# Attention and a gated FFN on one core: a planned order made anew, and queries loaded without their zeros

## Chip, cores and metric

The kernel runs on one core of a Trainium2 chip. The metric is the device time of one execution in microseconds. A core has five engines that run their own instruction streams and meet at semaphores: TensorE (PE in the profile, with its weight loads as PEld), VectorE (DVE), ScalarE (ACT), GpSimd (POOL) and SyncE (SP), which here only issues DMAs.

## What is computed

Two stages, all in float32. First a chunked attention over 4 batches, 8 heads, 768 positions and head size 64. Each chunk of 32 queries sees 16 positions to its left, its own 32, 8 to its right, and 8 memory keys shared by the head, so 64 keys. Then a feed-forward stage (FFN) with a gate: 512 to 1024 columns, ReLU, a convolution over three neighbouring positions, a sigmoid of it as the gate, and 1024 back to 512 columns.

```python
for c in range(nc):                      # 24 chunks of 32 queries
    k_full = concat([mem_k, k_ctx]); v_full = concat([mem_v, v_ctx])
    scores = scale * q_c @ k_full.T
    scores = scores - max(scores)
    a = exp(scores); a = a / (sum(a) + 1e-09)
    out[c] = a @ v_full
...
h = maximum(x @ w_in, 0.0)
conv_out = sum(conv_w[k] * hp[:, k:k + S, :] for k in range(3))
gate = 1.0 / (1.0 + exp(-conv_out))
return (h * gate) @ w_out
```

The FFN's weights come as float64, which the kernel reads as pairs of 32-bit words.

## The kernel before, in words

**An order written by a planner.** The function `attention_then_gated_ffn` doesn't emit instructions as it goes. It hands every operation to a `Plan` (`plan.op`, line 63): the engine, an assumed cost in ns, a due time, the code that emits it, what it reads and writes, and sometimes an ACT table (`exp` or `sigmoid`) or a mode of TensorE (`tiled` for the small matmuls of the attention, `whole` for the rest). `Plan.run` (line 99) then goes through time: of all operations that could start on an engine within a nanosecond of the earliest, it takes the one with the smallest due time, with `SWITCH` added where the operation needs another table than the one loaded and `MODE` where it changes TensorE's mode (line 150). It emits them in that order, one in-order stream for each engine and one for SP's DMA queue. The due times come from the table `DUE` (line 34): a start and a step for each group of operations. Costs and due times only set the order; what makes an instruction wait on the chip are its true dependences. Tiles come from rings of a few buffers each (`tile_of`, line 232), and a tile is handed out only when the planner has seen the last use of the buffer before it.

**Attention.** There are 32 steps `n` of the function `attention` (line 346): batch, half of the positions (`hf`, 12 chunks) and pair of heads (`cc`). One step: three loads (q, k, v), then 12 score matmuls of 64 stationary columns by 64 keys, one per chunk (line 384). Each stands in the profile as two instructions, so that a step has 24. The stationary operand holds a block diagonal: rows 0 to 63 are the first head and have its 32 queries in columns 0 to 31, rows 64 to 127 are the second head with columns 32 to 63, and the rest is zero. These zeros are in the array in device memory: `q_d` is loaded as 128 rows of 12 x 64 numbers (384 KB), with the 64 columns of a chunk side by side. Two chunks run beside each other in two column halves of the array (`j`). Then softmax: maximum on VectorE (line 393), subtract on VectorE (395), exp on ACT (397), edges set to zero (401, 403), sum, 1e-9 and reciprocal on VectorE (406 to 408), and the normalising product on GpSimd (413). Three transposes on TensorE (418), two copies by ACT into the block diagonal `a_d` (429), 12 matmuls with v (437, again two instructions each), and the result is split into a high and a low part, `x_hi` by ACT (446) and `x_lo` by VectorE (449). The first four steps take their q and k tiles from the ring `h`, later ones from rings of two.

**Weights.** `from_f64` (line 255) makes a high and a low float32 part of 128 x 512 float64 numbers. It has three recipes, chosen by a letter per block in `W_IN` and `W_OUT` (line 32): M works on VectorE (7 operations) and ACT, C on VectorE (6), ACT and one product on GpSimd, R on VectorE (4), ACT and three operations on GpSimd (316, 320, 325).

**FFN.** `ffn_in` (line 472 for its matmuls) takes, for each of 8 blocks of 128 hidden columns and each half of the positions, 12 matmuls of 384 columns; ACT applies the ReLU (488). `gate` (492) works per block on 128 x 768: the first tap of the convolution on ACT (498) or VectorE (502), two more on VectorE (508), the sigmoid on ACT (512), the product with h on VectorE or GpSimd (516). `split` (522) makes a high part by ACT (526) and a low part by VectorE or GpSimd (529). `ffn_out` (547) has 24 matmuls of 512 columns for each of 6 blocks of 128 positions and each batch, then a copy by ACT (559) and the store.

**Which engine does what.** Batch 0 has its first tap on ACT, and its product and low part in turn on GpSimd and VectorE. The other batches have tap and product on VectorE and the low part on GpSimd. All attention steps subtract on VectorE and normalise on GpSimd.

Of the kernel before, what the change touches and what calls it, by code (L numbers as in the profile page):

```python
# [22 lines left out]
NH = 2  # L23
NC = 12
# [3 lines left out]
TINY = 1.75 * 2.0**-15  # L28
WC = 512


W_IN, W_OUT = "MRRRCRMM", "MMRCMRMM"

DUE = {
    "w_in": (-1.1, 2.25), "w_in_load": (-15.9, 3.07), "w_out": (90, 0.44), "w_out_load": (55.6, 5.48),
# [4 lines left out]
    "gate": (25.7, 5.17)  # L40
# [10 lines left out]
class Plan:  # L51
# [47 lines left out]
    def run(self):  # L99
# [23 lines left out]
        for _ in range(n):  # L123
# [77 lines left out]
SWITCH, MODE = 1.9, 6.7  # L201
# [3 lines left out]
def attention_then_gated_ffn(  # L205
# [41 lines left out]

    w_in_p = [const.tile([P, NFC, NCC, P], F32R, name=f"w_in_{p}") for p in ("hi", "lo")]
# [6 lines left out]
    def from_f64(src, hi, lo, key, n, kind, due, first):  # L255

        w = tile_of("w64", 4, [P, WC, 2], U32)
# [88 lines left out]
    def attention(n, due):  # L346

        b, r = divmod(n, NU)
        hf, cc = divmod(r, NCC)

        q_d, k_t = (tile_of(*(("h", NFC) if n < 4 else (x, 2)), y) for x, y in (("q_d", [P, NC, 2 * CH]), ("k_t", [P, KC])))
        v_t = tile_of("v_t", 3, [P, NG, 2, 2, D])
        s, e, top, z = bank("s", 2), tile_of("e", 3, [P, 2 * NG, KW]), *(tile_of(x, 4, [P, 2 * NG]) for x in ("top", "z"))
# [4 lines left out]
        W = 2 * NG * KW  # L358
        s_ = lambda: s.t[:, :W].rearrange("p (g k) -> p g k", k=KW)
        over = lambda y: y.t.unsqueeze(2).broadcast_to([P, 2 * NG, KW])  # L360

        def load(tile, src, ahead):
            size = 1
            for x in src.shape:
                size *= x
            def do():
                flat = tile.t
                if len(flat.shape) == 3:
                    flat = flat.rearrange("p c q -> p (c q)")
                if len(flat.shape) == 5:  # L370
                    flat = flat.rearrange("p g c h d -> p (g c h d)")
                nc.sync.dma_start(out=flat, in_=src)
            plan.op("DMA", size * 4 / 300, due - DUE["load"][0] + ahead, do, w=(tile,))

        load(q_d, q[b, hf, cc], 0)
        load(k_t, k[b, hf, cc], 0)
        load(v_t, v[b, hf, cc], 1)

        def scores():
            for g in range(NG):  # L380
                for p in range(2):
                    for j in range(2):
                        c = 4 * g + 2 * j + p
                        nc.tensor.matmul(
                            s_()[j * D : (j + 1) * D, 2 * g + p, :],
                            lhsT=q_d.t[:, c],
                            rhs=k_t.t[:, c * STEP : c * STEP + KW],
                            start=True,
                            stop=True,
                        )  # L390

        plan.op("PE", 24 * 30, due, scores, (q_d, k_t), (s,), mode="tiled", late=250)
        plan.op("V", vec(W), due, lambda: nc.vector.tensor_reduce(out=top.t, in_=s_(), axis=AX.X, op=ALU.max), (s,), (top,))  # L393
        plan.op(
            "V", vec(W), due, lambda: nc.vector.tensor_tensor(out=e.t, in0=s_(), in1=over(top), op=ALU.subtract), (s, top), (e,)  # L395
        )
        plan.op("A", act(W), due, lambda: nc.scalar.activation(e.t, e.t, AF.Exp, scale=SCALE), (e,), (e,), table="exp")  # L397


        if hf == 0:  # L400
            plan.op("V", 80, due, lambda: nc.vector.memset(e.t[:D, 0, :LEFT], 0.0), (), (e,))
        if hf == NH - 1:
            plan.op("V", 80, due, lambda: nc.vector.memset(e.t[D:, 2 * NG - 1, KW - RIGHT :], 0.0), (), (e,))

        def total():
            nc.vector.tensor_reduce(out=z.t, in_=e.t, axis=AX.X, op=ALU.add)  # L406
            nc.vector.tensor_scalar_add(out=z.t, in0=z.t, scalar1=1e-9)  # L407
            nc.vector.reciprocal(out=z.t, in_=z.t)  # L408

        plan.op("V", vec(W) + 350, due, total, (e,), (z,))  # L410
        plan.op(
            "G", 2.15 * W, due,
            lambda: nc.gpsimd.tensor_tensor(out=e.t, in0=e.t, in1=over(z), op=ALU.mult), (e, z), (e,), shared=True,  # L413
        )

        def turn():
            for g in range(NG):
                nc.tensor.transpose(  # L418
                    out=t.t[:, g * P : (g + 1) * P],
                    in_=e.t[:, 2 * g : 2 * g + 2].rearrange("p g k -> p (g k)"),  # L420
                    identity=ident,
                )

        plan.op("PE", NG * 109, due, turn, (e,), (t,), mode="whole", late=250)
        for p in range(2):
# [5 lines left out]
            plan.op("A", act(W, True), due, place, (t,), (("a_d", p),))  # L431
# [155 lines left out]
    for n in range(4):  # L587
        attention(n, T_ATT[n])
# [3 lines left out]
    for n in range(4, 8):  # L592
        attention(n, T_ATT[n])
    tokens_in(0, (1,), *DUE["in0b"])
    for n in range(8, 12):
        attention(n, T_ATT[n])
    tokens_in(1, (0,), *DUE["in1a"])
    for n in range(12, 16):
        attention(n, T_ATT[n])
# [12 lines left out]
    y = [gate(fc, hs[1, fc][0], lin("gate1", fc), "V", "V", True) for fc in range(NFC)]  # L612
    g = [split(*y[fc], lin("split1", fc), "G") for fc in range(NFC)]
    for n in range(16, 24):
        attention(n, T_ATT[n])
    t = DUE["out"][0]
    def out_rest(b, g, t, last):
        for tt in range(3):
            ffn_out(b, g, tt, [t + 2.1 * fc + 0.1 * tt for fc in range(NFC)])
        for tt in range(3, 6):  # L620
            ffn_out(b, g, tt, [t + 17 + 5.7 * (tt - 3) + 0.7 * fc for fc in range(NFC)], 2 if last and tt == 5 else 1)
    out_rest(1, g, t, False)
    t += 34 + 8
    for b in range(2, B):
        tokens_in(b, (0, 1), t, 4.2)
        g = []
        for fc in range(NFC):
            y = gate(fc, hs[b, fc][0], t + lin("gate", fc), "V", "V")
            g.append(split(*y, t + lin("gate", fc), "G"))
        if b + 1 < B:  # L630
            for n in range((b + 1) * NU, (b + 2) * NU):
                attention(n, T_ATT[n])
# [6 lines left out]
def _laid_out(q, k, v, mem_k, mem_v):  # L639
# [19 lines left out]

    qt = q.reshape(B, H // 2, 2, NH, NC, CH, D).transpose(0, 3, 1, 2, 6, 4, 5)  # L660
    ql = np.zeros((B, NH, H // 2, 2, D, NC, 2, CH), q.dtype)
    for h in range(2):
# [50 lines left out]
```

## Time and profile before

| | |
|---|---|
| median of 3 runs | 371.07 us (370.65 to 371.46) |
| the profiled execution | 370.88 us |
| span of its instructions | 369.0 us |
| mean granted clock of TensorE in it | 0.982 |
| moved by DMA | 48.62 MB |
| ACT table loads | 22 of 1.283 us each |

The span runs from the first to the last instruction on the chip; the execution's time has 1.9 us around it. In the profile, "busy" of an engine is the time in which it had at least one instruction under way. Matmuls overlap one another, and the duration of a single one contains its latency: how fast they follow is read from the distance of their starts, not from their duration. "Idle before" of a group is time in which the engine stood empty just ahead of these instructions, and the name behind it is what released it.

### The profile page before, as it was taken

Reading aid. Unit: us, or ns where it says so; the run is one execution under the profiler, and the core shown is the slowest. Engines: PE = TensorE matmul, PEld = TensorE weight load, DVE = VectorE, ACT = ScalarE, POOL = GpSimd, SP = SyncE. Lnnn points to the kernel's source line nnn. Section 1 sums busy time; section 2 is a strip of 40 time slices with the busy share of each in tenths; the row PEclk is TensorE's granted clock in tenths of the full one; section 3 lists DMA queues with packets and bytes.
Section 4 is the critical chain, followed back from the end, with each engine's and each line's share of the span. In section 5 each row is a group of like instructions: output and inputs, shape, how many; then the busy total and the mean of one; then the engine's idle time right before and its main releaser. Section 6 shows DMA issues by size and latency. Waiting matters only on the chain.

```text
span 369.0 us, 7477 instructions
## 1 busy us (share of the span) xinstructions
PE 343.3 (93%) x3000; PEld 303.3 (82%) x3000; DVE 273.5 (74%) x444; ACT 212.4 (58%) x353; POOL 122.2 (33%) x155
## 2 busy tenths in 40 slices
PE   1577999999999999969999999999999999999996
PEld 1456999899999988857767899998868799998786
DVE  4979999999999999999995016999972117888300
ACT  4465777798755643879666127577594216453311
POOL 1665521244424354333542102254333002443300
PEclk9957999999999999999999999999999999999999
DMA  8988776844664000455643500413612100000021
GB/s 295 404 295 283 250 252 233 287 121 165 215 198 159 0 0 2 158 185 172 195 147 103 197 28 2 124 63 116 224 46 90 59 28 2 0 0 2 6 108 59
DMA packets 19907, 48.62 MB, mean 132 GB/s; under 512 B 2336, under 2 KB 6688, under 8 KB 19872
## 3 DMA queue, kind: packets, MB, share of 16 engines
q1 hardware_dynamic: 19872, 48.14, 38.1%
q8 instruction: 24, 0.39, 0.4%
q14 instruction: 11, 0.09, 0.1%
HBM read 41.84 MB, written 6.29 MB: 130 GB/s over the span
## 4 chain that ended last, share of the span: by engine, by line
DVE 54%; PE 28%; issue 6%; ACT 6%; POOL 3%; DMA 1%; POOLq 1%; DVEq 0%; ACTq 0%
PE f L547 16%; DVE c L508 14%; PE f L472 8%; DVE c L516 4%; DVE c L502 4%; DVE z L406 3%; DVE e L395 3%; DVE w_top L288 3%; DVE z L407 3%; DVE top L393 3%; PE a L437 3%; DVE x_lo L449 2%; DVE w L302 2%; DVE w_top L281 2%; DVE w L309 2%
## 5 line engine op out<-in xcount | busy, mean ns | idle before, releaser
L547 PE MATMUL f<-w_out_hi,g 128*128 128x512 f32 (+1 forms) x400 | 127.7, 392 | 0.3 <-POOL g L529 0.2
L472 PE MATMUL f<-x_hi,w_in_hi 128*128 128x384 f32 x256 | 89.1, 348 | 0.0
L547 PEld LDWEIGHTS f<-w_out_hi,g 128*128 128x128 f32 x400 | 74.0, 188 | 17.4 <-POOL g L529 1.6
L472 PE MATMUL f<-x_lo,w_in_hi 128*128 128x384 f32 x256 | 86.5, 338 | 0.0
L472 PE MATMUL f<-x_hi,w_in_lo 128*128 128x384 f32 x256 | 86.4, 338 | 0.0
L547 PE MATMUL f<-w_out_lo,g 128*128 128x512 f32 (+1 forms) x200 | 77.0, 385 | 0.0
L529 POOL TENSOR_TENSOR g<-c,g 128x768 fp32r<-128x768 f32 x20 | 40.4, 2018 | 96.1 <-ACT g L526 92.3
L508 DVE SCALAR_TENSOR_TENSOR c<-h,cw,c 128x768 f32<-128x768 f32 x48 | 62.2, 1296 | 1.6
L413 POOL TENSOR_TENSOR e<-e,z 128x384 f32<-128x384 f32 x32 | 30.0, 940 | 71.1 <-DVE z L408 26.3
L472 PEld LDWEIGHTS f<-x_hi,w_in_hi 128*128 128x128 f32 x256 | 48.6, 190 | 1.0
L472 PEld LDWEIGHTS f<-x_hi,w_in_lo 128*128 128x128 f32 x256 | 48.6, 190 | 0.1
L472 PEld LDWEIGHTS f<-x_lo,w_in_hi 128*128 128x128 f32 x256 | 48.4, 189 | 0.0
L547 PEld LDWEIGHTS f<-w_out_lo,g 128*128 128x128 f32 x200 | 37.6, 188 | 7.1
L502 DVE TENSOR_SCALAR c<-h,cw 128x768 f32<-128x768 f32 x24 | 21.7, 905 | 25.3 <-ACT h L488 25.3
L488 ACT ACTIVATE h<-f 128x384 f32<-128x384 f32 x48 | 23.5, 490 | 26.1 <-PE f L472 25.8
L437 PEld LDWEIGHTS a<-a_d,v_t 128*64 128x64 f32 x768 | 26.6, 144 | 12.9 <-issue 6.4
L512 ACT ACTIVATE c<-c 128x768 f32<-128x768 f32 x32 | 27.1, 846 | 17.0 <-DVE c L508 16.8
L559 ACT COPY o_sb<-f 128x512 f32<-128x512 f32 (+1 forms) x25 | 14.0, 569 | 38.0 <-PE f L547 26.6
L437 PE MATMUL a<-a_d,v_t 128*64 128x64 f32 x768 | 30.9, 233 | 4.5 <-ACT a_d L429 2.6
L429 ACT COPY a_d<-t 64x384 f32<-64x384 f32 x64 | 30.2, 472 | 5.8 <-PE t L418 5.1
L449 DVE TENSOR_TENSOR x_lo<-a,x_hi 128x384 fp32r<-128x384 f32 x32 | 17.3, 542 | 16.3 <-ACT x_hi L446 16.1
L397 ACT ACTIVATE e<-e 128x384 f32<-128x384 f32 x32 | 16.8, 524 | 20.7 <-DVE e L395 19.8
(63 smaller groups left out, 439.9 us busy)
## 6 DMA issues: line engine op xcount, KB each, us to landing
v_t<-in_v_dram SPq DMA_DIRECT2D x32, 384.0 KB, 3.7
q_d<-in_q_dram SPq DMA_DIRECT2D x28, 384.0 KB, 5.2
k_t<-in_k_dram SPq DMA_DIRECT2D x28, 252.0 KB, 5.3
out_dram<-o_sb SPq DMA_DIRECT2D x23, 256.0 KB, 2.0
w<-in_w_in_dram SPq DMA_DIRECT2D x8, 512.0 KB, 5.1
w<-in_w_out_dram SPq DMA_DIRECT2D x8, 512.0 KB, 4.0
h<-in_q_dram SPq DMA_DIRECT2D x4, 384.0 KB, 6.4
h<-in_k_dram SPq DMA_DIRECT2D x4, 252.0 KB, 6.4
```

The costliest lines, as they stand in the source:

```text
L397: plan.op("A", act(W), due, lambda: nc.scalar.activation(e.t, e.t, AF.Exp, scale=SCALE), (e,), (e,), table="exp")
L413: lambda: nc.gpsimd.tensor_tensor(out=e.t, in0=e.t, in1=over(z), op=ALU.mult), (e, z), (e,), shared=True,
L429: nc.scalar.copy(out=a_d[r, :, p, :], in_=t.t[r, : NG * P].rearrange("p (g q) -> p g q", q=CH))
L437: nc.tensor.matmul(a.t[h * D : (h + 1) * D, g * P + j * D : g * P + (j + 1) * D], lhsT=v_t.t[:, g, j, h], rhs=a_d[:, 4 * g + 2 * j + h].re ...
L449: lambda: nc.vector.tensor_tensor(out=x_lo.t[:, cc], in0=a.t[:, :TW], in1=x_hi.t[:, cc].bitcast(F32), op=ALU.subtract),
L472: nc.tensor.matmul(f.t[:, :TW], lhsT=w_in_p[c][:, fc, cc], rhs=x_p[a].t[:, cc], start=(m == 0), stop=(m == 3 * NCC - 1),)
L488: nc.scalar.activation(h.t[:, 1 + o : 1 + o + TW], f.t[:, :TW], AF.Relu)
L502: lambda: nc.vector.tensor_scalar(out=c.t, in0=h.t[:, 0:S], scalar1=w[0], scalar2=None, op0=ALU.mult),
L508: lambda i=i: nc.vector.scalar_tensor_tensor(out=c.t, in0=h.t[:, i : i + S], scalar=w[i], in1=c.t, op0=ALU.mult, op1=ALU.add), (*H, c), (c ...
L512: plan.op("A", act(S), due, lambda: nc.scalar.activation(c.t, c.t, AF.Sigmoid), (c,), (c,), table="sigmoid")
L529: lambda: (nc.vector if lo == "V" else nc.gpsimd).tensor_tensor(out=g_lo(), in0=x(), in1=g_hi().bitcast(F32), op=ALU.subtract), (h, p[0]), ...
L547: nc.tensor.matmul(ps.t[:, :n], lhsT=g[fc][a].t[:, tt * P : (tt + 1) * P], rhs=w_out_p[c][:, fc, o : o + n], start=(fc == 0 and i == 0), s ...
```

## The change

*Queries.* The zeros are no longer in device memory. `queries` loads each step's two heads as two DMAs of 64 rows, 96 KB each, into the two blocks of a tile `[P, 2, CH, NC]` whose other blocks are set to zero by GpSimd. From the fifth step on there are two such tiles, zeroed once and used in turn; the first four steps take tiles of the ring `h`, each zeroed by itself. The chunk is now the innermost index, so that the 64 stationary columns of a chunk, `q_t()[:, :, :, c]`, stand 12 numbers (48 bytes) apart.

*Softmax.* By the letters of `SOFT`, 13 of 32 steps no longer subtract on VectorE: VectorE multiplies the six maxima by -scale, and ACT does six exps of 64 columns straight from the scores' bank, with the maximum as bias. By `NORM`, 17 of 32 steps normalise on VectorE, the other 15 on GpSimd.

*Gate.* The letters of `TAP`, `MULT` and `LO` choose the engine of the first tap (24 ACT, 8 VectorE; before 8 and 24), of the product (19 GpSimd, 13 VectorE; before 4 and 28) and of the low part (12 GpSimd, 20 VectorE; before 28 and 4) for each block of each batch.

*Weights.* `W_IN` and `W_OUT` have other letters.

*Order.* All due times are new. `SWITCH` goes from 1.9 to 64.1 and `MODE` from 6.7 to 32.4, and the planner's cost for a change back to whole matmuls from 250 to 120 ns. The three operations between sum and reciprocal are separate entries now. The change also allows steps to be worked in pairs (`PAIRS`, `GROUP`), but every group has one step.

```diff
-W_IN, W_OUT = "MRRRCRMM", "MMRCMRMM"
+W_IN, W_OUT = "MRCCCCMM", "RRRRMMCC"
+TAP = "AVVAAAAVAAAAAAVAAVAVVVAAAAAAAAAA"
+MULT = "GVVVVGGVGGGGGVVVVGGVVGGGVGGGVGGG"
+LO = "GGVGVVGVVVVGGGVVVVVVVGGVVGGVVVGV"
+SOFT = "VAVVVAAAAAAAVVVAVVVVVAVVVVVAAVVA"
+NORM = "VGGGGGGGGGGVGGGGVVVVVVVVVVVVVVGV"
+GROUP = "11111111"
 DUE = {
-    "w_in": (-1.1, 2.25), "w_in_load": (-15.9, 3.07), "w_out": (90, 0.44), "w_out_load": (55.6, 5.48),
-    "load": (11.3, 6.35), "att0": (1.5, 0), "att1": (13.3, 3.09), "att2": (23.5, 4.11), "att3": (68.2, 4.75),
-    "att4": (134.9, 6.29), "att6": (222.1, 6.59), "in0a": (16.2, 1.93), "in0b": (48.4, 3.05),
-    "in1a": (66.7, 2.68), "in1b": (88.8, 1.97), "gate0": (73.5, 8.41), "out0": (103.6, 0.84),
-    "out0b": (136.8, 2.94), "gate1": (167.1, 0), "split1": (148.2, 7), "out": (169.8, 0.83),
-    "gate": (25.7, 5.17)
+    "w_in": (-0.3, 2.09), "w_in_load": (-19.8, 9.87), "w_out": (51.2, 2.77), "w_out_load": (51.2, 19.2),
+    "load": (4.9, 2.04), "att0": (-2.8, 0), "att1": (-2.5, 5.14), "att2": (27.1, 4.41), "att3": (49.2, 4.44),
+    "att4": (142.6, 7.91), "att6": (217.8, 5.47), "in0a": (22.9, 0.55), "in0b": (74.4, 0.42),
+    "in1a": (114.4, 1.22), "in1b": (120.2, 1.59), "gate0": (71.8, 6.93), "out0": (151.7, 0.66),
+    "out0b": (138.3, 0), "gate1": (133.1, 5.76), "split1": (124.6, 12.08), "out": (192.1, 2.65),
+    "gate": (68.9, 9.63)
 }
...
-                cost += 95 if md == "tiled" else 250
+                cost += 95 if md == "tiled" else 120
...
-SWITCH, MODE = 1.9, 6.7
+PAIRS = False
+SWITCH, MODE = 64.1, 32.4
...
+    q_d = [const.tile([P, 2, CH, NC], F32, name=f"q_d{i}") for i in range(2)]
+    for x in q_d:
+        nc.gpsimd.memset(x[:D, 1], 0.0)
+        nc.gpsimd.memset(x[D:, 0], 0.0)
...
+                def less(i=i, s_=s_):
+                    for g in range(2 * NG):
+                        nc.scalar.activation(
+                            part(e, i)[:, g], s_()[:, g], AF.Exp, bias=part(top, i)[:, g : g + 1], scale=SCALE
+                        )
...
+            plan.op(
+                norm, vec(W) if norm == "V" else 2.2 * W, due,
+                lambda i=i: (nc.vector if norm == "V" else nc.gpsimd).tensor_tensor(
+                    out=part(e, i), in0=part(e, i), in1=part(z, i).unsqueeze(2).broadcast_to([P, 2 * NG, KW]), op=ALU.mult
+                ), ((e, i), z), ((e, i),), shared=True,
+            )
...
+    def queries(n, b, hf, cc, due):
+        if n < 4:
+            tile = tile_of("h", NFC, [P, 2, CH, NC])
+            get, key = (lambda: tile.t), tile
+            def zeros():
+                nc.gpsimd.memset(tile.t[:D, 1], 0.0)
+                nc.gpsimd.memset(tile.t[D:, 0], 0.0)
+            plan.op("G", 840, due, zeros, w=((tile, 2),))
+        else:
+            get, key = (lambda: q_d[n % 2]), ("q_d", n % 2)
+        for h in range(2):
+            r = slice(h * D, (h + 1) * D)
+            plan.op(
+                "DMA", D * TW * 4 / 300, due,
+                lambda r=r, h=h: nc.sync.dma_start(out=get()[r, h].rearrange("p q c -> p (q c)"), in_=q[b, hf, cc, r]),
+                w=((tile, h),) if n < 4 else (("q_d", n % 2, h),),
+            )
...
-                            s_()[j * D : (j + 1) * D, 2 * g + p, :],
-                            lhsT=q_d.t[:, c],
+                            s.t[j * D : (j + 1) * D, o : o + KW],
+                            lhsT=q_t()[:, :, :, c].rearrange("p h q -> p (h q)"),
                             rhs=k_t.t[:, c * STEP : c * STEP + KW],
...
-        y = gate(fc, hs[0, fc][0], due, "A", "GV"[fc % 2])
-        g.append(split(*y, due, "VG"[fc % 2]))
+        g.append(split(*through_gate(0, fc, due), due, LO[fc]))
...
-    ql = np.zeros((B, NH, H // 2, 2, D, NC, 2, CH), q.dtype)
-    for h in range(2):
-        ql[:, :, :, h, :, :, h] = qt[:, :, :, h]
+    ql = q.reshape(B, H // 2, 2, NH, NC, CH, D).transpose(0, 3, 1, 2, 6, 5, 4).reshape(B, NH, H // 2, 2 * D, CH * NC)
```

More of the change, by code (lines that the diff above doesn't have):

```diff
@@ new lines, in scores, with mm @@
+    def scores(s, q_t, q_k, k_t, due):
+        def mm():
+            for g in range(NG):
+                for p in range(2):
+                    for j in range(2):
+                        c = 4 * g + 2 * j + p
+                        o = (2 * g + p) * KW
+                        nc.tensor.matmul(
+                            s.t[j * D : (j + 1) * D, o : o + KW],
+                            lhsT=q_t()[:, :, :, c].rearrange("p h q -> p (h q)"),
+                            rhs=k_t.t[:, c * STEP : c * STEP + KW],
+                            start=True,
+                            stop=True,
+                        )
+        plan.op("PE", 24 * 30, due, mm, (*q_k, k_t), (s,), mode="tiled", late=250)
@@ L348, in attention, with outcome @@
+    def outcome(n, v_t, e, i, due):
         b, r = divmod(n, NU)
         hf, cc = divmod(r, NCC)
-        q_d, k_t = (tile_of(*(("h", NFC) if n < 4 else (x, 2)), y) for x, y in (("q_d", [P, NC, 2 * CH]), ("k_t", [P, KC])))
-        v_t = tile_of("v_t", 3, [P, NG, 2, 2, D])
-        s, e, top, z = bank("s", 2), tile_of("e", 3, [P, 2 * NG, KW]), *(tile_of(x, 4, [P, 2 * NG]) for x in ("top", "z"))
         t, a = bank("t", 1), bank("a", 1)
@@ L357, in attention @@
         x_hi, x_lo = x_of[b, hf]
[L358 to L373, printed above, removed]
@@ L392, in attention @@
[L392 to L401, printed above, removed]
@@ L402, in attention @@
[L402 to L414, printed above, removed]
@@ L586, in attention_then_gated_ffn, with steps, through_gate @@
     T_ATT += [lin("att3", i) for i in range(4)] + [lin("att4", i) for i in range(8)] + [lin("att6", i) for i in range(8)]
-    for n in range(4):
-        attention(n, T_ATT[n])
+    def steps(i, n):
+        while i < n:
+            size = GROUP[i // 4] == "2" and i % 2 == 0 and 2 or 1
+            attention(range(i, i + size), T_ATT[i : i + size], SOFT[i], NORM[i])
+            i += size
+    def through_gate(b, fc, due, keep=False):
+        i = b * NFC + fc
+        return gate(fc, hs[b, fc][0], due, TAP[i], MULT[i], keep)
+    steps(0, 4)
     for fc in range(NFC):
@@ L611, in attention_then_gated_ffn @@
         ffn_out(0, g, tt, [lin("out0b", fc) + 0.1 * tt for fc in range(NFC)])
[L612 to L615, printed above, removed]
+    y = [through_gate(1, fc, lin("gate1", fc), True) for fc in range(NFC)]
+    g = [split(*y[fc], lin("split1", fc), LO[NFC + fc]) for fc in range(NFC)]
+    steps(16, 24)
     t = DUE["out"][0]
@@ L627, in attention_then_gated_ffn @@
         for fc in range(NFC):
-            y = gate(fc, hs[b, fc][0], t + lin("gate", fc), "V", "V")
-            g.append(split(*y, t + lin("gate", fc), "G"))
+            due = t + lin("gate", fc)
+            g.append(split(*through_gate(b, fc, due), due, LO[b * NFC + fc]))
         if b + 1 < B:
-            for n in range((b + 1) * NU, (b + 2) * NU):
-                attention(n, T_ATT[n])
+            steps((b + 1) * NU, (b + 2) * NU)
         out_rest(b, g, t + 34, b + 1 == B)
```

100 lines of the change are left out of this document (74 added, 26 removed).

## The prediction, made before the changed kernel was run

> **What bounds the kernel now.** I read the page first: the engines' totals and the span in forty slices.
>
> ```profile
> span 369.0 us, 7477 instructions
> PE 343.3 (93%) x3000; PEld 303.3 (82%) x3000; DVE 273.5 (74%) x444; ACT 212.4 (58%) x353; POOL 122.2 (33%) x155
> ...
> PE   1577999999999999969999999999999999999996
> ...
> DVE  4979999999999999999995016999972117888300
> ```
>
> TensorE (PE) is the engine that matters: from the fifth slice on it is nearly always busy, while VectorE (DVE) is full from the fourth to the twenty-second slice and has room after that. All work of TensorE is needed, so time can come only from its empty places, from its changes between kinds of work, or from what one piece of its work costs. To place the empty time I cut the span at the points where the kind of work changes (columns: stretch, its length, busy time of PE, PEld, DVE, ACT and POOL, then the granted clock, the DMA share and GB/s).
>
> ```profile
> 0.00:7.80 7.80, 0.00 (x0) 0.00 (x0) 3.23 (x7) 3.81 (x5) 1.38 (x7) 1.00 0.78 275
> 7.80:32.80 25.00, 15.64 (x255) 13.44 (x256) 21.14 (x55) 12.79 (x27) 14.43 (x14) 0.77 0.92 333
> 32.80:41.00 8.20, 8.19 (x101) 7.63 (x99) 7.89 (x18) 6.37 (x13) 2.71 (x7) 0.86 0.72 222
> 41.00:150.00 109.00, 108.15 (x1000) 99.65 (x997) 104.54 (x179) 72.67 (x128) 40.42 (x58) 1.00 0.46 157
> 150.00:206.00 56.00, 52.17 (x535) 40.96 (x534) 47.23 (x76) 41.12 (x61) 22.52 (x21) 1.00 0.51 172
> 206.00:346.00 140.00, 139.58 (x1012) 125.13 (x1011) 89.45 (x114) 71.60 (x114) 38.85 (x48) 1.00 0.17 57
> 346.00:369.00 23.00, 19.59 (x107) 16.46 (x105) 0.00 (x0) 4.05 (x8) 1.84 (x1) 1.00 0.19 69
> ```
>
> [...] **The start (17 us) and 150 to 206 (4 us) are all there is to win by order.** What is waited for there, by the waits view, first of 7.8 to 41 us, then of 150 to 206 us:
>
> ```profile
> PEld t L418 <- POOL e L413: 6.3, 3, 2.9
> ```
> ```profile
> PEld t L418 <- POOL e L413: 4.3, 5, 1.7
> ```
>
> In both stretches PE's largest wait (the first leaves out the first loads) is the transpose of the attention weights, waiting for the normalisation that GpSimd (POOL) does. The end of the start, from the timeline, shows an in-order queue as well:
>
> ```profile
> 31.40 0.83 POOL L413 TENSOR_TENSOR e<-e,z 128x384 f32<-128x384 f32 x1 [1.81 <-DVE w_top L281]
> 31.77 0.52 ACT L397 ACTIVATE e<-e 128x384 f32<-128x384 f32 x1 [1.53 <-DVE e L395]
> 32.28 0.90 PE L418 MATMUL t<-ident,e 128*128 128x128 f32 x3 [2.73 <-POOL e L413]
> 32.32 0.48 ACT L446 CAST x_hi<-a 128x384 fp32r<-128x384 f32 x1
> ```
>
> The last x_hi that the first FFN matmul needs comes from ACT at 32.32, behind an exp (31.77) that stood 1.53 us waiting for VectorE; PE stood 2.73 us.
>
> **The change, part by part.** The groups of instructions give the prices (columns: line, engine, operation, tiles, count | busy us, mean ns | idle before):
>
> ```profile
> L498 ACT ACTIVATE c<-g,cw 128x768 f32<-128x768 f32 x8 | 7.4, 935 | 0.1
> L502 DVE TENSOR_SCALAR c<-h,cw 128x768 f32<-128x768 f32 x24 | 21.7, 905 | 25.3 <-ACT h L488 25.3
> L395 DVE TENSOR_TENSOR e<-s,top 128x384 f32<-128x384 f32 x32 | 17.8, 555 | 1.8 <-PE t L418 0.3
> L397 ACT ACTIVATE e<-e 128x384 f32<-128x384 f32 x32 | 16.8, 524 | 20.7 <-DVE e L395 19.8 <-DVE e L401 0.6
> L488 ACT ACTIVATE h<-f 128x384 f32<-128x384 f32 x48 | 23.5, 490 | 26.1 <-PE f L472 25.8
> L294 ACT CAST cw_hi<-w_top 128x24 fp32r<-128x24 f32 x1 | 0.2, 214 | 0.0
> L413 POOL TENSOR_TENSOR e<-e,z 128x384 f32<-128x384 f32 x32 | 30.0, 940 | 71.1 <-DVE z L408 26.3 <-DVE x_lo L449 9.3 <-ACT g L488 9.1
> L320 POOL TENSOR_TENSOR w_top<-w_top,w 128x512 f32<-128x512 f32 x6 | 7.9, 1319 | 0.4
> L325 POOL TENSOR_TENSOR w_in_lo<-w_top,w_in_hi 128x512 fp32r<-128x512 f32 x4 | 5.4, 1354 | 2.5 <-ACT w_in_hi L322 2.5
> ```
>
> *Engines.* By the letters, taps on VectorE fall from 24 to 8: 16 x 0.905 = 14.5 us off DVE, 16 x 0.935 = 15.0 us onto ACT. Seventeen of 32 normalisations go from POOL to DVE: 17 x 0.94 = 16.0 us off POOL, and 17 x 0.555 (the subtract of the same shape) = 9.4 us onto DVE. The two 768-wide products of the gate only change places: 32 on POOL before, 31 after. Thirteen steps take max off inside ACT's exp: 13 x 0.555 = 7.2 us off DVE, less a scaling of six columns, which I take at the 0.21 us of the smallest row here, and six activations of 64 columns in place of one of 384. Between 0.214 us (24 columns) and 0.490 us (384) a 64-column one is about 0.25 us, so 1.5 us for 0.52 us, +13 us on ACT. Together DVE loses 14.5 + 7.2 - 2.8 - 9.4 = about 10 us of 273, ACT gains some 28 of 212, and POOL loses 14 to 16 of 122. ACT at 240 is still two thirds of the span; table loads, which the new SWITCH weight puts off, I leave at no change. None of this is PE time, so by itself it is worth nothing outside the stretches with empty PE.
>
> *The start.* In the first four weight blocks the recipe M R R R becomes M R C C. An R gives POOL three products, a C only the first of them: two blocks without L320 and L325 are 2 x (1.32 + 1.35) = 5.3 us less of the 14.4 us on POOL, whose products stand in line ahead of the normalisations that the transposes wait for. The first step's normalisation goes to DVE, and the due times put the first four steps (-2.8) ahead of the first weight block (-0.3), where before two weight blocks came first. Against it: step 4 is due at -2.5, also ahead of that block, and DVE is 85% busy. The queries' half saves 192 KB ahead of the first scores, at 275 GB/s 0.7 us. Best case: all 9.4 + 0.7 = 10.1 us; worst: another wait as long as the longest here, +2.9 us. I take -4.0, a little over a third of the empty time, because half the wait view's transposes (6.3 us) should go with POOL's queue and the rest hangs on DVE, which is not relieved here.
>
> *150 to 206.* All eight steps of the third batch normalise on DVE. Their 4.3 us of PE waits end with POOL's queue; the next to be late is DVE itself, busy 47 of 56 us, since here five products leave it and five subtractions of the same shape come, so that only 7 taps less 8 normalisations relieve it (7 x 0.905 - 8 x 0.555 = 1.9 us). I take -2.0 of the 3.8 us empty; bounds -3.8 and +3.8 (as much again).
>
> *Changes of kind.* The rows of the next fence show 48 score matmuls in one block from 39.55 to the next matmul at 41.05, 1.50 us, while a block of 24 alone takes 45.41 to 46.26, 0.85 us: joining two saves 0.2 us. MODE goes from 6.7 to 32.4, so more blocks should join; if five of the 64 groups of 24 join one that they didn't before, -1.0, bounds -3 and 0.
>
> *Zeros and loads.* From the timeline, POOL's one large memset, a query load and the first v loads as SP issues them, and the first matmuls that read v:
>
> ```profile
> 1.25 0.74 POOL L246 MEMSET a_d<- 128x768 f32 x1
> ...
> 1.64 0.42 SPq L372 DMA_DIRECT2D h<-in_q_dram  x1
> ...
> 7.72 1.99 SPq L372 DMA_DIRECT2D v_t<-in_v_dram  x3
> ...
> 17.74 1.30 PE L437 MATMUL a<-a_d,v_t 128*64 128x64 f32 x24
> ```
>
> Twelve half-tile memsets on POOL, half of L246 each, are 12 x 0.37 = 4.4 us. The four for the lasting tiles and the two for step 0 end 2.2 us after L246, at 4.2, before the first scores at 7.8: hidden under the loads. Without that cover each would delay the scores by 0.37. Each step has one DMA more on SP's queue, 0.42 us to issue. Behind the four extra ones of the start stand the v loads, 1.7 us later than 7.72, and those are first read at 17.74. I take 0; bound +2.
>
> *The stationary columns.* This is the price that the trace doesn't hold: in every load of weights there the columns are adjacent. The rows: blocks at full clock, the stretch around 20.5 us with its clock of 0.50 and a block in it, load groups of 64 and 128 columns, and the only strided reads there are (ACT reading every second word, L273, beside the same width unstrided, L294).
>
> ```profile
> 39.55 1.57 PE L384 MATMUL s<-k_t,q_d 128*64 128x64 f32 x48
> ...
> 41.05 0.44 PE L472 MATMUL f<-x_hi,w_in_hi 128*128 128x384 f32 x1
> ...
> 45.41 0.92 PE L437 MATMUL a<-a_d,v_t 128*64 128x64 f32 x24
> 46.26 0.44 PE L472 MATMUL f<-x_hi,w_in_hi 128*128 128x384 f32 x1
> ```
> ```profile
> 20.40:22.00 1.60, 1.52 (x25) 1.41 (x25) 1.20 (x3) 0.03 (x1) 0.19 (x1) 0.50 1.03 376
> ...
> 20.48 1.55 PE L437 MATMUL a<-a_d,v_t 128*64 128x64 f32 x24 [1.44 <-ACT a_d L429]
> ```
> ```profile
> L472 PEld LDWEIGHTS f<-x_hi,w_in_hi 128*128 128x128 f32 x256 | 48.6, 190 | 1.0
> ...
> L384 PEld LDWEIGHTS s<-k_t,q_d 128*64 128x64 f32 x672 | 22.2, 143 | 0.7 <-issue 0.7
> ...
> L273 ACT ACTIVATE w_top<-w 128x512 f32<-128x512 f32 (+1 forms) x17 | 11.1, 650 | 4.5 <-DMA w<-in_w_in_dram 3.0 <-POOL w_out_lo L325 0.5 <-POOL w_in_lo L325 0.5
> ...
> L294 ACT CAST w_out_hi<-w_top 128x512 fp32r<-128x512 f32 x6 | 3.7, 620 | 5.3 <-DVE w_top L288 5.3
> ```
>
> 64 columns more cost a load 190 - 143 = 47 ns, and matmuls on the two column halves of the array go in pairs, 1.50 us / 24 = 62 ns each: the load fits with 15 ns to spare. From below: 0, if a strided load is as fast. From above: everything at half speed, the block at half clock, 1.55 - 0.92 = 0.63 us a step, 32 x 0.63 = 20 us. The nearest row, the same load unstrided, says 0, and the strided read on ACT costs 5%, 2 ns of 47; I take **0**, and keep +20.
>
> [...]
>
> **The sum.** -4.0 - 2.0 - 1.0 = -7.0 us. The profiled execution took 370.9 us, 1.9 outside its span; the median of the runs is 371.1, so I predict **364.0**.
>
> **Rivals.** (1) *The strided load is the bound* of the score blocks. With half the rate a load takes 94 ns, and a pair about 94 instead of 62: 32 ns x 12 pairs x 32 steps = 12 us; by the half-clock block 20. A few steps lie in the start's empty time, so +15: 379. It decides once a load takes over 62 ns, and eats the whole gain at 62 + 7.0 us / 384 = 80 ns. For it: only 15 ns of cover. Against: nothing measured. Chance 0.27. (2) *The new order makes as many waits as it removes*: DVE stays over 80% busy from 8 to 200 us, ACT's six-part exp holds a score bank 1 us longer in the start, and with x as late as before the time is 370 (368 to 373). For it: PE's waits follow whichever engine is late, and 13 us more exp stand in ACT's in-order queue, which already cost 1.5 us at 31.77. Against: POOL, the releaser of the largest waits, is the engine relieved. Chance 0.20. (3) *The start is cleared better than I take*: FFN matmuls from 26 instead of 32.8, full clock with it, 357. Chance 0.08, and 0.45 for the forecast, 360 to 368.
>
> **Chances and range.** About 0.2% is what a measurement of this kernel can tell from no change. Faster: 0.45 + 0.08 + 0.08 of rival 2 + 0.02 of rival 1 = 0.63; same 0.08; slower 0.29. The forecast's own range is 359 to 368; for 8 in 10, with rival 1 up to its lower half and a little beyond, 356 to 381.
>
> **What would show it.** First FFN matmul at 28 to 29 us instead of 32.8; a PE wait for POOL's e under 3 us in the start and under 1 after 150; PE busy in the stretches from 40 us to the end close to full; a lone score block of 24 still 0.85 us and its loads 143 ns. A block of 1.2 us or more shows rival 1, and the forecast is wrong by that. An FFN start at 32 or later, or new waits for DVE and ACT of 5 us, shows rival 2.

## The result: slower by 3.3%, and the profile after

| | before | after |
|---|---|---|
| median, same chip | 371.26 us (370.65 to 371.69, 4 runs) | 383.25 us (382.94 to 385.14, 4 runs) |
| ratio after to before | | 1.0332, 95% interval 1.0299 to 1.0364 |
| the profiled execution | 370.88 us | 385.14 us |

The forecast was 364.0 with a range of 356 to 381: wrong in sign, and outside its range by 2 us. From here on the price of a part is worked out from the difference of two ratios, each to the kernel before on the same chip, times 371.3 us; after is then +12.3 us. Times and ratios are of fast runs: one run of the loads split by rows (381.51 us) and one of the old weight letters (371.51 us) were in a slow state and are left out. The profiled execution of after is the slowest of its runs, so sums from its profile come out some 2 us larger than the 12.3.

The page of after, its engines' totals and two lines of the span in forty slices:

```profile
span 383.2 us, 7592 instructions
PE 365.8 (95%) x3000; PEld 329.5 (86%) x3000; DVE 260.0 (68%) x445; ACT 226.6 (59%) x427; POOL 109.2 (29%) x150
...
PE   1869999999999999999999999999999999999996
...
DVE  4788998887997998997984466679831005598000
```

PE has the same 3000 matmuls and is busy 22.5 us longer, and its weight loads 26.2 us longer. The other engines moved the way that the change says: DVE lost 13.5 us, ACT gained 14.2 (half of the forecast's 28, since its table loads, 1.283 us each, fell from 22 to 12), POOL lost 13.0. The span grew by 14.2. So the change did take out waiting, and something made the matmuls themselves dearer. The stretches of after say where PE is empty (columns as before: stretch, length, busy PE, PEld, DVE, ACT, POOL, clock, DMA share, GB/s):

```profile
0.00:8.40 8.40, 0.00 (x0) 0.00 (x0) 3.78 (x7) 3.72 (x5) 7.08 (x19) 1.00 0.79 218
8.40:34.70 26.30, 21.14 (x303) 19.04 (x303) 20.60 (x56) 14.25 (x37) 8.72 (x9) 0.94 0.98 272
44.00:158.00 114.00, 113.41 (x989) 105.43 (x986) 101.64 (x172) 79.74 (x159) 44.94 (x59) 1.00 0.40 124
150.00:206.00 56.00, 56.00 (x435) 46.32 (x434) 49.29 (x73) 40.79 (x63) 17.12 (x17) 1.00 0.37 115
```

After the start almost nothing is empty: 0.6 us of 114, and none at all from 150 to 206, where before had 3.8 us. In the start 5.2 us are empty (26.30 - 21.14) in place of 9.4 (25.00 - 15.64), and yet the first FFN matmul comes at 34.74 in place of 32.83. What fills that time is in the page's groups:

```profile
L478 PE MATMUL s<-k_t,q_d 128*64 128x64 f32 x672 | 48.7, 300 | 2.2 <-DMA k_t<-in_k_dram 1.8
L478 PEld LDWEIGHTS s<-k_t,q_d 128*64 128x64 f32 x672 | 46.9, 236 | 3.1 <-issue 2.4
...
L518 PEld LDWEIGHTS a<-a_d,v_t 128*64 128x64 f32 x768 | 25.6, 140 | 9.6 <-issue 4.4
```

The loads of the score matmuls of steps 5 to 32 took 22.2 us before, 143 ns each; now 46.9 us, 236 ns each. The loads of the matmuls with v, with as many columns but side by side, take 140 ns (144 before). And a block of 24 score matmuls by itself, from the timeline:

```profile
84.59 1.78 PE L478 MATMUL s<-k_t,q_d 128*64 128x64 f32 x24
86.31 0.55 PE L499 MATMUL t<-ident,e 128*128 128x128 f32 x3
```

1.72 us from its first matmul to the next instruction, where the forecast wanted 0.85 and named 1.2 and more as the sign of rival 1, the strided load as the bound. (The block of 0.85 that it showed is one of matmuls with v; a lone score block of before, at 153.39 us, takes 0.80.) PE counts as busy in all of this (56.00 of 56 us from 150 to 206): the longer blocks look like work in the totals, and only the price of one shows them.

The distance of starts is the better measure. I add up, from each matmul's start to the next one's, all distances by the kind of the first (so a wait counts with the kind ahead of it), in us of the profiled executions:

| | first scores | scores | transposes | with v | FFN in | FFN out |
|---|---|---|---|---|---|---|
| before | 7.84 | 30.2 | 13.8 | 31.2 | 139.2 | 143.3 |
| after | 8.46 | 55.7 | 16.0 | 26.2 | 136.6 | 136.8 |

Scores +25.5, everything else -11.9, first scores +0.6: the 14.2 us by which the span grew.

### The profile page after: what moved, and what is told of

Read it like the earlier page. It is cut to its first block, busy times and chain, and to the rows that moved or that the text cites. A ratio compares the mean times of both kernels' runs of the same rounds, so it can differ in the third digit from the quotient of the medians.

```text
span 383.2 us, 7592 instructions
## 1 busy us (share of the span) xinstructions
PE 365.8 (95%) x3000; PEld 329.5 (86%) x3000; DVE 260.0 (68%) x445; ACT 226.6 (59%) x427; POOL 109.2 (29%) x150
## 4 chain that ended last, share of the span: by engine, by line
PE 86%; DMA 7%; DVE 5%; issue 1%; SPq 1%; ACT 0%; ACTq 0%; DVEq 0%
PE f L628 36%; PE f L553 32%; PE s L478 10%; PE a L518 6%; DMA h<-in_q_dram 3%; PE t L499 2%; DMA k_t<-in_k_dram 2%; DMA v_t<-in_v_dram 2%; DVE w L319 1%; DVE w_top L305 1%; DVE w L314 1%; DVE w_top L298 0%; DVE x_lo L530 0%; DVE w_top L293 0%; DVE top L387 0%
## 5 line engine op out<-in xcount | busy, mean ns | idle before, releaser
L553 PE MATMUL f<-x_hi,w_in_hi 128*128 128x384 f32 x256 | 87.9, 343 | 0.0
L589 DVE SCALAR_TENSOR_TENSOR c<-h,cw,c 128x768 f32<-128x768 f32 x48 | 63.6, 1332 | 24.5 <-ACT c L579 23.4
L597 POOL TENSOR_TENSOR c<-c,h 128x768 f32<-128x768 f32 x11 | 20.3, 1852 | 129.9 <-ACT c L593 129.9
L478 PE MATMUL s<-k_t,q_d 128*64 128x64 f32 x672 | 48.7, 300 | 2.2 <-DMA k_t<-in_k_dram 1.8
L478 PEld LDWEIGHTS s<-k_t,q_d 128*64 128x64 f32 x672 | 46.9, 236 | 3.1 <-issue 2.4
L518 PEld LDWEIGHTS a<-a_d,v_t 128*64 128x64 f32 x768 | 25.6, 140 | 9.6 <-issue 4.4
L518 PE MATMUL a<-a_d,v_t 128*64 128x64 f32 x768 | 29.9, 229 | 2.2 <-ACT a_d L510 2.2
L387 DVE TENSOR_REDUCE top<-s 128x6 f32<-128x384 f32 x32 | 17.6, 551 | 17.4 <-PE s L478 17.2
```

The source lines that it names most:

```text
L387: lambda i=i, s_=s_: nc.vector.tensor_reduce(out=part(top, i), in_=s_(), axis=AX.X, op=ALU.max), (s,), ((top, i),),
L478: nc.tensor.matmul(s.t[j * D : (j + 1) * D, o : o + KW], lhsT=q_t()[:, :, :, c].rearrange("p h q -> p (h q)"), rhs=k_t.t[:, c * STEP : c * ...
L518: nc.tensor.matmul(a.t[h * D : (h + 1) * D, g * P + j * D : g * P + (j + 1) * D], lhsT=v_t.t[:, g, j, h], rhs=a_d[:, 4 * g + 2 * j + h].re ...
L553: nc.tensor.matmul(f.t[:, :TW], lhsT=w_in_p[c][:, fc, cc], rhs=x_p[a].t[:, cc], start=(m == 0), stop=(m == 3 * NCC - 1),)
L589: lambda i=i: nc.vector.scalar_tensor_tensor(out=c.t, in0=h.t[:, i : i + S], scalar=w[i], in1=c.t, op0=ALU.mult, op1=ALU.add), (*H, c), (c ...
L597: lambda: (nc.vector if mult == "V" else nc.gpsimd).tensor_tensor(out=y(), in0=c.t, in1=h.t[:, 1 : S + 1], op=ALU.mult), (c, h), (h if kee ...
```

## The experiments

The theory after the result: columns 48 bytes apart make the score blocks twice as long; the new order by itself gains what the forecast said. The rivals: the new order loses too, or the new loads do.

### The stationary columns alone, in the kernel before

```diff
-        q_d, k_t = (tile_of(*(("h", NFC) if n < 4 else (x, 2)), y) for x, y in (("q_d", [P, NC, 2 * CH]), ("k_t", [P, KC])))
+        q_d, k_t = (tile_of(*(("h", NFC) if n < 4 else (x, 2)), y) for x, y in (("q_d", [P, 2 * CH, NC]), ("k_t", [P, KC])))
...
-                            lhsT=q_d.t[:, c],
+                            lhsT=q_d.t[:, :, c],
```

The array in device memory is laid out to match; order, loads and bytes stay.

> The kernel before with its order, its loads (384 KB with the zeros) and its engines, and only the stationary columns of the scores 48 bytes apart (the block diagonal is laid out with the chunk innermost). If the stride alone slows the score matmuls as in the changed kernel (a lone block of 24 from 0.85 to 1.71 us, two together from 1.50 to 3.34): 0.86 to 0.92 us x 32 steps = 27 to 29 us, less a few steps in the start's empty time, so 371.3 + 22 to 29 = 393 to 400 us. If the slower blocks come from something else in the change (loads in two halves, zeroed tiles, neighbours in the new order): 370 to 374 us and blocks of 0.85 us.

Measured: 388.31 us, ratio 1.0448 (1.0420 to 1.0476), +16.6 us. The stride alone loses more than the whole change does, so the rest of the change gains. But the loss is smaller than expected. The page's row of the loads, then the stretch from 150 to 206:

```profile
L384 PEld LDWEIGHTS s<-k_t,q_d 128*64 128x64 f32 x672 | 46.9, 236 | 0.7 <-issue 0.7
```
```profile
150.00:206.00 56.00, 55.93 (x492) 46.11 (x491) 49.84 (x72) 41.24 (x59) 21.09 (x13) 1.00 0.44 141
```

The load is dearer by as much as in after. By distances of starts the scores take 55.3 us, +25.1, but FFN out takes 5.5 us less (137.8) and the other kinds 2.1 less together. The second row shows why: before, PE stood 3.8 us between 150 and 206, waiting for GpSimd's normalisation; with longer score blocks GpSimd is done in time, and PE stands 0.1 us. A dearer piece of PE's work is partly paid from waits that PE had anyway.

### Six distances of the columns in one kernel

Step `n` (counted from 0) takes a column distance of 1, 2, 3, 4, 6 or 12 numbers by `n` modulo 6; all else is the kernel before.

```diff
+WS = (1, 2, 3, 4, 6, 12)
...
-                            lhsT=q_d.t[:, c],
+                            lhsT=q_d.t.rearrange("p (a q w) -> p a q w", q=2 * CH, w=WS[n % 6])[:, c // WS[n % 6], :, c % WS[n % 6]],
```

> The kernel before with another distance of the stationary columns in each step, by the step's number modulo 6: 4, 8, 12, 16, 24 and 48 bytes; same instructions, same loads. Read from it are the score blocks of each distance, not the total. [...] If every step to another address beyond the next costs alike: 8 bytes is as slow as 48. If the price grows with the distance: 16 well below 48.

Two of its places in the timeline; the first block holds the seventh and the eighth step (4 and 8 bytes), the second the two after them (12 and 16 bytes), and each is followed by the next matmul:

```profile
39.85 1.59 PE L385 MATMUL s<-k_t,q_d 128*64 128x64 f32 x48
41.37 0.44 PE L473 MATMUL f<-x_hi,w_in_hi 128*128 128x384 f32 x1
...
52.39 2.66 PE L385 MATMUL s<-k_t,q_d 128*64 128x64 f32 x48
54.98 0.44 PE L473 MATMUL f<-x_hi,w_in_hi 128*128 128x384 f32 x1
```

1.52 us and 2.59 us. (This kernel ran once, in 377.10 us; only its blocks are read.) The score matmuls start in pairs, some 7 ns apart, which the forecast reads as one in each column half. For each step alone I take the distance between the starts of every second score matmul, so of one pair and the next, its median in the blocks at full clock. What it takes more than at 4 bytes stands beside it:

| column distance | a pair, ns | more than at 4 bytes, ns |
|---|---|---|
| 4 bytes | 58 | |
| 8 bytes | 60 | 2 |
| 12 bytes | 88 | 30 |
| 16 bytes | 120 | 62 |
| 24 bytes | 113 to 115 | 55 to 57 |
| 48 bytes | 134 to 135 | 76 to 77 |

Up to 16 bytes the price rises with the distance, by 2 ns from 4 to 8, 28 from 8 to 12 and 32 from 12 to 16. Beyond 16 it doesn't follow the distance: 24 bytes take 5 to 7 ns less than 16, and 48 take 14 to 15 more. So 8 bytes (60) are nowhere near as slow as 48 (134), and 16 (120) are not well below 48. From 16 bytes on a pair takes about twice what it takes with adjacent columns; by which mechanism is not shown.

### All of the change with adjacent columns, and with 8 bytes

The order, the engines, the zeroed tiles and the half loads of after; only the layout inside the query tile differs, with `WQ` 1 (adjacent, runs of 128 bytes in the load) and 2 (8 bytes apart, runs of 256).

```diff
-    q_d = [const.tile([P, 2, CH, NC], F32, name=f"q_d{i}") for i in range(2)]
+    q_d = [const.tile([P, NC // WQ, 2, CH, WQ], F32, name=f"q_d{i}") for i in range(2)]
...
-                            lhsT=q_t()[:, :, :, c].rearrange("p h q -> p (h q)"),
+                            lhsT=q_t()[:, c // WQ, :, :, c % WQ].rearrange("p h q -> p (h q)"),
```

> The changed kernel, every instruction in the same order on every engine, but the tile of the queries is laid out chunk by chunk, so that the 64 stationary columns of a chunk are adjacent; the two loads of each step then write runs of 128 bytes in place of 1536. If the stride is the whole loss and the order, engines and loads are a gain: 383.3 - 27 = 356 us (352 to 361). If the order brings no gain by itself: 368 or more. If short runs make the loads late: waits of the scores for the query loads of over 5 us in total, and above 361.

> [...] If any stride costs: up to 383.

Measured: 369.96 us, ratio 0.9950 (0.9930 to 0.9970), and 369.19, ratio 0.9934 (0.9908 to 0.9960). Columns 8 bytes apart do as well here as adjacent ones: the intervals of the two ratios overlap. But the size misses the expectation by 8 us and more: without the stride the change gains only 2.5 us, and the whole of it isn't explained by the stride. By the waits of PE from 8 to 45 us (first of the adjacent columns, then of 8 bytes), the scores wait for loads:

```profile
PE s L482 <- DMA h<-in_k_dram: 12.6, 4, 9.4
```
```profile
PE s L482 <- DMA h<-in_k_dram: 10.6, 3, 9.0
```

The longest of each is the wait ahead of the first scores (9.4 and 9.0 us, 7.84 before); the others come between the scores of the start. The first FFN matmul stands at 35.2 us with 8 bytes, not at 28 to 29. So either the new order doesn't clear the start, or the new loads fill it up again.

### The order alone, and the loads alone

One kernel has after's order and engines with the query loads of before (one DMA of 128 rows, zeros included, adjacent columns, no memsets); its main lines against after are shown. The other has before's order with the new loads (8 bytes apart).

```diff
+            def one(h=h):
+                if h == 0:
+                    nc.sync.dma_start(out=get().rearrange("p c q -> p (c q)"), in_=q[b, hf, cc])
...
-                lambda r=r, h=h: nc.sync.dma_start(out=get()[r, h].rearrange("p q c -> p (q c)"), in_=q[b, hf, cc, r]),
+                one,
```

> The changed kernel's order, engines and letters, every planned operation in the same place, but the old loads: one DMA of 384 KB a step with the zeros, adjacent columns, no memsets. This is the order alone. If the new loads make the start late: first scores at 7.8 to 8.2, first FFN matmul at 33 to 34, and 1 to 2 us below the run with columns 8 bytes apart (369.2), 367 to 368. If the order itself makes the start late: first FFN matmul still at 35, and 369 to 371; with twice the bytes in flight even a little above.

> The kernel before in its planned order, only with the new loads: two DMAs of 64 rows a step into zeroed tiles, columns 8 bytes apart (which the run of strides showed at 60 ns a pair against 58). If these loads are what makes the start late (first scores at 8.5 to 9.4 us in all runs that have them, 7.8 in before): first scores at about 9, and 0.5 to 2.5 us above before, 372 to 374. If half the bytes are worth what the prediction took: first scores at 7.1, and 370 to 371. Of the total some 0.6 us is the 8 bytes themselves (2 ns x 12 x 32 = 0.8).

Measured: the order alone 365.84 us, ratio 0.9852 (0.9824 to 0.9880), -5.5 us; the new loads alone 373.08, ratio 1.0037 (1.0020 to 1.0055), +1.4 us. The order gains more than was expected of it after the result, and nearly what the forecast took; its stretches:

```profile
3.00:15.00 12.00, 5.57 (x96) 4.95 (x96) 9.28 (x20) 4.40 (x11) 2.32 (x2) 1.00 1.02 397
7.90:29.30 21.40, 14.89 (x303) 12.75 (x304) 19.38 (x54) 13.26 (x35) 7.99 (x9) 1.00 1.03 395
150.00:206.00 56.00, 54.35 (x571) 44.35 (x570) 45.64 (x81) 37.49 (x62) 12.58 (x14) 1.00 0.51 171
```

The first FFN matmul stands at 29.30. The clock column says 1.00, where before had 0.77 up to 32.8 and 0.86 up to 41, but it doesn't tell all of the start: pairs of the first three score blocks, up to 12.4 us, take 107 ns, as they do in before at a granted clock of 0.50, and 58 ns from 13.45 us on. From 150 to 206 PE is empty 1.65 us in place of 3.83. Some of that is given back just behind the start; PE's waits from 40 to 52 us:

```profile
PE f L552 <- POOL w_in_lo L346: 1.8, 2, 1.2
PE f L552 <- DVE w_in_lo L351: 0.9, 1, 0.9
PE f L552 <- ACT w_in_hi L308: 0.7, 1, 0.7
```

3.4 us, all for converted weights: the FFN matmuls start earlier and catch up with the conversion, which by the new due times is planned behind the first four attention steps.

### Why the new loads are slow: their halves

In the new loads several things are new: half the bytes, two DMAs in place of one, shorter runs, 64 rows in place of 128, and GpSimd's zeroing of the tiles ahead of them. The stretch from 3 to 15 us, in which the first scores wait for loads, first of before, then of before's order with the new loads:

```profile
3.00:15.00 12.00, 4.93 (x96) 4.40 (x96) 9.94 (x25) 4.10 (x7) 3.79 (x4) 1.00 1.03 402
```
```profile
3.00:15.00 12.00, 4.69 (x74) 4.25 (x75) 9.13 (x18) 4.02 (x7) 8.20 (x13) 1.00 1.15 253
```

The DMA engines are full in both (a share of 1.03 and 1.15), but move 402 GB/s in the one and 253 in the other. To part them, two kernels with the order alone load the old bytes in two DMAs each: once split by rows (runs of 3072 bytes as before), once by columns (128 rows, runs of 1536 bytes).

```diff
+                r = slice(h * D, (h + 1) * D)
+                nc.sync.dma_start(out=get()[r].rearrange("p c q -> p (c q)"), in_=q[b, hf, cc, r])
```
```diff
+                x = slice(h * NC * CH, (h + 1) * NC * CH)
+                nc.sync.dma_start(out=get().rearrange("p c q -> p (c q)")[:, x], in_=q[b, hf, cc][:, x])
```

> The run of the order alone (old loads with zeros, adjacent columns; 365.8), with one thing changed: each query load is issued as two DMAs of 64 rows, same bytes, same runs, no memsets. If the number of DMAs on SP's queue makes the start late (two halves took 1.2 to 1.6 us to issue where one load took 0.4 to 0.5): first scores at 8.6 to 9.1 us in place of 7.95, the fourth k load issued at 9 to 9.5 in place of 5.7, and 367.5 to 369.5 in total. If it is GpSimd's memsets or the shorter runs of the new loads: first scores within 0.3 us of 7.95, and 365 to 366.8.

> The order alone with each query load cut the other way: two DMAs of all 128 rows and half the columns, 192 KB each, runs of 1536 bytes (cut by rows, two DMAs of 64 rows and runs of 3072 bytes gave 376.2 and moved 289 GB/s from 3 to 15 us, where the uncut loads moved 397). If it is the 64 rows that move slowly: 380 to 400 GB/s there, first scores at 8.0 to 8.5, and 366 to 368. If it is the number of DMAs, whatever their shape: about 290 GB/s, first FFN matmul at 36 or later, and 373 to 377.

Measured: split by rows 375.60 us, ratio 1.0112 (1.0081 to 1.0142), 9.7 us over the order alone, several times what was expected; split by columns 365.60, ratio 0.9849 (0.9818 to 0.9881), no different from it. The same stretch, rows first:

```profile
3.00:15.00 12.00, 4.65 (x72) 4.17 (x72) 7.30 (x16) 4.29 (x11) 1.17 (x2) 1.00 1.04 289
```
```profile
3.00:15.00 12.00, 6.20 (x96) 5.54 (x96) 9.47 (x21) 4.41 (x11) 2.32 (x2) 1.00 1.04 387
```

Neither the number of DMAs nor the length of the runs, but the 64 rows: with both halves of a tile on their way one behind the other, the full DMA engines move 289 GB/s in place of 397. By rows the first FFN matmul comes at 37.8 us, by columns at 30.8. In after half of the bytes are gone and the loss is smaller (3.0 us for the new loads against 9.7), but the rate is no better (251 GB/s in its stretch from 3 to 15 us). GpSimd's zeroing isn't the cause of the late start either: the kernel split by rows has none and starts its scores at 8.45, as after does at 8.46, where step 1's own zeros are done at 4.58. In all kernels that load the first steps in row halves the scores start between 8.45 and 9.35 us, in all others between 7.46 and 7.95.

Waiting is only half of the 7.0 us between the two FFN starts: up to there PE's empty time is 3.5 us longer by rows, and its busy time 3.5 as well. A score block from each timeline, rows first, shows the second part:

```profile
33.00 1.55 PE L477 MATMUL s<-k_t,q_d 128*64 128x64 f32 x24 [0.92 <-DMA k_t<-in_k_dram]
```
```profile
26.68 0.92 PE L477 MATMUL s<-k_t,q_d 128*64 128x64 f32 x24
```

By rows the pairs of score matmuls still take 107 ns at 33 us, by columns 58 from 26.68 us on, and the clock column says 1.00 in both places. So PE stays at the pace of half clock for longer where it starts late. That the waits for loads hold it there is not shown.

If this is a matter of the start, where loads are waited for, the half loads should cost nothing later. One more kernel takes the old loads for steps 1 to 4 and the new ones (8 bytes) for the other 28:

```diff
+                if n < 4:
+                    if h == 0:
+                        nc.sync.dma_start(out=get().rearrange("p c q -> p (c q)"), in_=q[b, hf, cc])
+                    return
```

> The changed order; steps 0 to 3 with the old loads, steps 4 to 31 with the new ones (halves without zeros, columns 8 bytes apart, lasting zeroed tiles). If the new loads cost only at the start: first scores at 8.0, first FFN matmul at 29 to 30, and 365.5 to 367 (0.7 us for the columns). If they cost wherever they stand: 367 to 369.5.

Measured: 366.61 us, ratio 0.9864 (0.9844 to 0.9883), 0.4 us from the order alone and inside its interval. Twenty-eight of 32 steps with the new loads cost nothing that can be told; the four at the start cost 2.6 us (0.9934 less 0.9864, against the kernel with 8 bytes in all steps). Its first FFN matmul stands at 30.87 us.

### One engine's move alone

In the kernel before, the normalisation of the last 16 steps goes from GpSimd to VectorE.

```diff
-            "G", 2.15 * W, due,
-            lambda: nc.gpsimd.tensor_tensor(out=e.t, in0=e.t, in1=over(z), op=ALU.mult), (e, z), (e,), shared=True,
+            "V" if n >= 16 else "G", vec(W) if n >= 16 else 2.15 * W, due,
+            lambda: (nc.vector if n >= 16 else nc.gpsimd).tensor_tensor(out=e.t, in0=e.t, in1=over(z), op=ALU.mult), (e, z), (e,), shared=True,
```

> The kernel before, with one of the change's moves alone: the 16 attention steps of the last two batches normalise on VectorE in place of GpSimd. If the middle (150 to 206 us) was empty because transposes waited in GpSimd's queue: those waits (4.3 us of PE) fall below 1.5 us, PE's empty time there from 3.8 to below 2, and 368.5 to 370 in total. If VectorE, busy 47 of 56 us there, is late in its place: waits for DVE of 2 us or more appear, and 371 to 373.

Measured: 368.17 us, ratio 0.9911 (0.9887 to 0.9936), -3.3 us. The stretch from 150 to 206:

```profile
150.00:206.00 56.00, 55.53 (x575) 44.57 (x574) 49.80 (x90) 43.23 (x65) 16.05 (x14) 1.00 0.56 188
```

0.5 us empty in place of 3.8: nearly the whole gap was the wait for GpSimd, and VectorE at 49.8 of 56 us doesn't take its place.

### An attempt on the new wait

The order alone with the old letters for the first weights, `W_IN` `MRRRCRMM`, to see whether the 3.4 us of waits for converted weights go.

> The run of the order alone (365.8) with the weight recipes of before, MRRRCRMM in place of MRCCCCMM: GpSimd has three products more in blocks 2, 3 and 5, VectorE two operations fewer in each; the planner makes its order with that. PE there waited 3.7 us for converted weights between 40 and 52 us. If VectorE is what is late: these waits under 1.5 us, and 362 to 364.5. If GpSimd's queue is: waits for its w_in products as long as now or longer, and 365.5 to 368.

Measured: 367.85 us (365.01 to 368.86 over 9 runs), ratio 0.9882 (0.9854 to 0.9910), which overlaps that of the order alone. The planner's order changes with the letters, so this isn't the recipe alone; where its time goes was not followed up. No gain, and it says nothing more. The order alone, with its query loads whole or in column halves, is the fastest version found, 1.5% below the kernel before.

## Why the prediction was wrong, point by point

The parts as measured, in us against before: order and engines -5.5, new loads (with columns 8 bytes apart) +3.0, columns 48 bytes apart in place of 8 +14.8 (1.0332 less 0.9934), together +12.3. In before's order the same two parts cost +1.4 and +16.6.

**The stationary columns: the step that failed.** The forecast took 0 and kept 20 as the upper bound. It had the mechanism as rival 1, with a chance of 0.27, and two of its readings were wrong. The choice of 0 leaned on the same load unstrided and on ACT's strided read, 5% dearer; that read takes every second word, 8 bytes apart, and at 8 bytes the table above has 2 ns more a pair, at 48 bytes 76. And the block at half clock was no upper bound: in the half-clock stretch of before a pair takes 107 ns, of the strided kernel 134 (the fifth step of both, at 26 us, granted clock 0.50), while at full clock it is 58 and 134. The strided pair doesn't follow PE's clock, so "everything at half speed" bounds another thing. The full price, (134 - 58) ns x 384 pairs, is 29 us; four steps of before go at 107 ns, which takes 2.4 us off it, and the sums of starts, which hold waits too, grow by 25.1; and 16.6 (before's order) or 14.8 (after's) reach the end. What is missing was paid from PE's waits. That the end moved by less than the bound of 20 is luck: PE's own price is above it. Rival 1's number, +15, thus came out near right by luck, from two errors against each other: too cheap a pair (94 ns) and no waits to pay from but the start's. No run shows the half rate that it supposes for the load, which was the author's estimate: the mean of the loads went from 143 to 236 ns, the pair from 58 to 134.

**Zeros and loads: the second one.** Taken at 0 with a bound of +2, and with 0.7 us of gain counted for half the bytes in the start's best case. Measured: +3.0 (each ratio has some 1 us either way). The step counted issues and bytes, and not the rate: it read 275 GB/s before the first scores and supposed that it stays. The first scores came 0.6 us later (8.46), not 0.7 earlier. Its issues were too cheap too: two halves hold SP's queue for 1.1 to 1.5 us where one load takes 0.4 to 0.5; but the column halves, 0.9 to 1.6 us a pair, cost nothing, so that isn't the price. What the runs show is a rate: from 3 to 15 us, 289 GB/s with the loads split by rows against 397 with whole ones, with other loads, of 128 rows, between them. Why loads of 64 rows move less is not shown; the rate of the halves alone isn't measured, nor how much of the +3.0 is the rate and how much PE's lower pace behind it.

**The start: right in the main.** Forecast -4.0 and a first FFN matmul at 28 to 29; with the old loads it stands at 29.30, and at 30.80 and 30.87 in the two kernels with the same order and the same time (query loads in column halves, new loads from the fifth step on): 2.0 to 3.5 us earlier than in before. PE's empty time up to there falls by about 2.8, 4.6 and 4.8 us. The earliest of the three starts is in part its pace: its score pairs take 58 ns from 13.45 us on, those of the other two still 107 at 21 us. Not foreseen: the wait of 3.4 us for converted weights behind it. The chance that the new order makes as many waits as it removes (rival 2) thus held for a part of the gain. That full clock comes with an earlier start, as rival 3 has it, was the author's estimate, and what grants the clock is not shown: in before it was 1.00 from 12 to 16 us with PE busy for 1.61 of 4.00, and 0.50 from 24 to 28 us with 3.97 of 4.00. In after itself, with the other two parts, the first FFN matmul came at 34.74, the forecast's sign for rival 2, though the order isn't what delayed it.

**150 to 206: right.** Forecast -2.0, the empty time fell by 2.2 in the order alone and by 3.4 where only the normalisation was moved. In after no wait of PE for POOL's e is left there, as the forecast's test wanted.

**Changes of kind: the -1.0 is not shown.** Counted from the trace, the changes between tiled and whole matmuls went from 63 to 67, the wrong way. A greater `MODE` sets only the planner's preference; blocks didn't join more often. With a lone score block of 0.80 us, joining two saves 0.1 us and not 0.2. What the four changes more cost wasn't measured.

**The sum.** Of -7.0, -5.5 came true for the parts that the sum spoke of, not broken down further; the two that it put at nothing cost 17.8.

Left open: whether a pair's 134 ns are two loads one behind the other or two beside each other; why a pair takes 120 ns at 16 bytes, 114 at 24 and 134 at 48; why PE's pace stays low for longer behind late loads; and what a better due time for the weights' conversion would give on top of the order alone.

## What to carry to other kernels

Before laying a stationary operand out with gaps, time one block at that distance: float32 columns 4 and 8 bytes apart took 58 and 60 ns a pair here, 12 bytes 88, and 16 to 48 bytes 113 to 135, about double. A price that the trace lacks shouldn't be taken from the row that looks nearest, but from the one that shares the mechanism; where none does, it belongs in the forecast with its full bound. Leaving zeros out of a load saved nothing here, where each load then covered only 64 of 128 rows: at the start, where the scores wait for loads, four steps of it cost 2.6 us.

## What the runs showed of the hardware

- A pair of score matmuls with stationary columns 48 bytes apart took the same at a granted clock of 0.50 and of 1.00 (134 ns), one with adjacent columns 107 and 58.
- With columns 4, 8, 12 and 16 bytes apart a pair took 58, 60, 88 and 120 ns; with 24 bytes 114, with 48 bytes 134.
- From 3 to 15 us, loads split by rows moved 289 GB/s at a DMA share of 1.04, by columns 387 at the same share: the busy share of the DMA engines didn't tell their rate.
- The profile's clock column can say 1.00 where TensorE goes at half pace: at the start, score pairs with adjacent columns took 107 ns under it, up to 12.4 us in one run and past 33 us in another. The distance of pairs tells the pace.
